# Attention with a routed expert layer: the rest of the routing ahead of the next expert's splits, two early transposes moved, and register loads placed elsewhere

## The chip, the core and the metric

The kernel runs on one core of one Trainium2 chip. A core has a matrix engine (TensorE, "PE" in the profile; its weight loads are "PEld"), VectorE ("DVE"), ScalarE ("ACT"), GpSimd ("POOL") and SyncE ("SP"), which here issues most transfers. Each engine runs its own queue in order and waits for the others by semaphores. The metric is the device time of one execution in microseconds (us); lower is better.

## What is computed

Block attention over 4 batches, 8 heads, 768 positions and 64 channels gives x of 3072 rows and 512 columns. Each row is then sent to one of 8 experts, a two-layer network with 1024 hidden columns. The cut reference of that second part:

```python
logits = x @ w_gate                       # 8 experts
local_gate = sigmoid(x @ w_local)
for b in range(B):
    prev_e = -1
    for s in range(S):
        fresh_e = argmax(logits[b, s])
        e = fresh_e if s == 0 or local_gate[b, s] < 0.5 else prev_e
        prev_e = e
        p = softmax(logits[b, s])
        h = maximum(x[b, s] @ w1[e], 0)
        out[b, s] = p[e] * (h @ w2[e])
```

The expert of a row is known only at run time, so the kernel sorts rows by expert while it runs.

## The kernel before

**Slots.** Rows are sorted into slots of 128 rows, all of one expert. Slots 0 to 5 (`EARLY` = 6) are filled from the first batch alone, with its commonest expert, so that their work can begin before the routing of the other batches is known. Up to 38 more follow, and two small slots of at most 32 rows (the "few" path) whose first and last matrices are loaded plain into the tile `raw`. A slot's rows are fetched by an indirect transfer that GpSimd issues (`gather`, L1030, tile `xg`), transposed by TensorE (L1041, in `tx`) and split by ScalarE and VectorE into a high and a low part (`split_ps`, L1034 and L1036, tile `xT`). Results are scaled by the gate value `psort` and scattered by GpSimd (L1083).

**Matmuls.** Every product is made of three: high by high, high by low, low by high. `pair` does two slots (first layer L1180 to L1182, 12 matmuls per 128 hidden columns), `quad` four (L1197 to L1199). The second layer, `second`, is a loop of blocks (slots) and 8 steps each; a step is three matmuls of 512 columns (L1059 to L1061). Steps are counted over all blocks: 0 to 15 in a pair, 0 to 31 in the quad. Behind a step the function may call `mids[step]`, and at steps given by `PW1` and `PW2` the functions that replace the weights by those of the next expert: ScalarE rounds (L1013, tile `h`), VectorE and GpSimd subtract (L1016 and L1021, tile `l`); when a matrix is through, SyncE reloads its staging tile `stg` (L1008). In the first pair `PM0` names the steps of the transposes of slots 2 to 5; in the quad `PM4` those of slots 6 to 9, counted from 18.

**Routing.** `route`, `finish` and `rows` are generators of small VectorE instructions. They end in `words`, a row of integers on one partition that say which slot begins a new expert, which expert it is, and how many slots there are. Last of all comes `bp` (L995): three products of the one-hot tile `eqp` with the three parts of the gate values, then 24 matmuls with `A` (L999) and a sum (L1002) that give `psort` for slots 6 onward. A sibling of the L999 matmuls, L908, gives the rows' addresses.

**What sets the order.** The program is written out in one order, which fixes each engine's own. While the first pair and the quad are written, `flow` is called behind each step: it keeps an estimate of TensorE's and VectorE's time and gives out a routing instruction when, by that estimate, it would not start too early. `small(n)` instead gives out VectorE instructions for a credit of n at once, stopping at one for TensorE unless told otherwise. Each weight split adds 1.4 us to VectorE's estimated time (`self.dve(1.4)` in `split`), so routing behind it is given out later.

**Reading words.** `reg` (L1324, through `values_load`) makes each named engine load one word into a register (TENSOR_LOAD in the trace); conditions are taken on it. The words on the two small slots are loaded by all engines behind the quad (`some`), and the number of slots (`nb`) before the last slots.

Of the kernel before, what the change touches and what calls it, by code (L numbers as in the profile page):

```python
# [32 lines left out]
KT, FT = DM // P, DF // P  # L33
# [8 lines left out]
SLOTS = 44  # L42
# [2 lines left out]
FEW = 32  # L45
FEWS = 2
COLS = SLOTS + FEWS
FEW_AT = ((1, 26, 29, 36, 40, 57), (37, 59, 62, 76, 80, 98))
OOB = 4096
WARM = 44  # L50
# [11 lines left out]

SPLIT_BY = ("VGVV", "VGVG")

PM, PM0, PM4 = (2, 5), (3, 6, 11, 14), (18, 21, 24, 27)
PW1, PW2 = (0, 2, 4, 6), (10, 12, 14, 15)

ON_PE = {"PE": 2, "PE late": 4, "ACT": 4}
# [9 lines left out]
class Kernel:  # L78
    def __init__(self, ctx, tc, qT, kT, vT, vW, maskc, identc, wgc, w1, w2, c32c, cb16c, out):
# [46 lines left out]
        self.zero = cst.tile([P, P], F32, name="zero")  # L126
        self.words = cst.tile([1, 2 * COLS + 1], I32, name="words")
        self.gidx = cst.tile([P, COLS], I32, name="gidx")
        self.sidx = cst.tile([P, COLS], I32, name="sidx")
        self.psort = cst.tile([P, COLS], F32, name="psort")  # L130
        self.wz = cst.tile([P, P], BF16, name="wz")
# [653 lines left out]
    def finish(self):  # L785
# [191 lines left out]
        for i in range(2):  # L977
            nc.tensor.matmul(out=m[0:1, COLS * i:COLS * i + COLS], lhsT=w2[:, i:i + 1], rhs=self.ident[:, 0:COLS],
                             start=True, stop=True)
        yield "DVE"  # L980
        v.tensor_copy(out=self.words[:, 2 * COLS:], in_=tot)
        yield "DVE"
# [259 lines left out]
    def run(self):  # L1242
# [45 lines left out]
        def freed():  # L1288
            st["free"] += 1
            ask_rows()  # L1290
# [6 lines left out]
        def block0():  # L1297
            self.mw2 = self.pool("m_wk2")
            self.w2c = ExitStack()
            self.w2b = self.w2c.enter_context(tc.tile_pool(name="w2b", bufs=1))  # L1300
            self.xT = self.mw2.tile([P, KT, 2, 4, P], F32R, name="xT")
            self.hT = [self.mw2.tile([P, FT, 2, 2 * P], F32R, name="hT0")]
            for i in range(2):
                while st["next"] <= i:
                    self.small(1, True)
                    ask_rows()
                self.tx(i, "s")
                freed()
                yield
# [13 lines left out]
        def reg(i, engines, hi):  # L1323
            return nc.values_load(self.words[0:1, i:i + 1], engines=engines, min_val=0, max_val=hi)  # L1324

        def refill(w, nxt):

            with tc.If(nxt > 0):
                e = nc.s_assert_within(nxt - 1, 0, E - 1, skip_runtime_bounds_check_because="the branch is taken for 1 to E alone")
                for h in range(2):  # L1330
                    self.fetch(st["stage"][w][:, 2048 * h:2048 * h + 2048], w, 2048 * h, 2048 * h + 2048, e)

        def split(w, chunks):
            for q in chunks:
                eng = nc.vector if SPLIT_BY[w][q] == "V" else nc.gpsimd
                self.split(w, q * CH, q * CH + CH, st["stage"][w][:, q * CH:q * CH + CH], eng)

        def calls(n, mids={}):

            r = {}  # L1340

            def start(s):
                while "words" not in st:
                    self.small(1, True)
                if s not in r:
                    r[s] = reg(s, (ENG.SP, ENG.Activation, ENG.DVE, ENG.Pool), 1), reg(COLS + s, (ENG.SP,), E)
                return r[s]

            def weights(w, s, chunks):
                if not EARLY <= s < SLOTS:  # L1350
                    return
                new, nxt = start(s)
                with tc.If(new > 0):  # L1353
                    split(w, chunks)
                    if chunks[-1] == NCH - 1:
                        refill(w, nxt)

            def turn(u):
                while st["next"] <= u:
                    self.small(1, True)  # L1360
                if u % 2 and u >= 2 * PAIRS:
                    with tc.If(reg(u, (ENG.PE, ENG.Activation, ENG.DVE), 1) > 0):
                        self.tx(u)
                else:
                    self.tx(u)
                freed()

            mids = {j: lambda u=u: turn(u) for j, u in mids.items() if u < SLOTS}
            return mids, lambda *chunks: weights(0, n, chunks), lambda *chunks: weights(1, n, chunks)
# [11 lines left out]
        first = chain(block0(), self.pair(0, *calls(2, dict(zip(PM0, range(2, 6))))))  # L1381
# [5 lines left out]
        with ExitStack() as ctx:  # L1387
# [31 lines left out]
                        p = slice(2048 * h, 2048 * h + 2048)  # L1419
                        self.fetch(self.raw[:, p], w, p.start, p.stop, e)  # L1420

            rest = chain(first, self.quad(2, *calls(6, dict(zip(PM4, range(6, 10))))))
            while self.steps:
                next(rest, None)
                self.flow(C_T)
# [5 lines left out]
            self.raw = lw.tile([P, KT * DF], F32, name="raw")  # L1431
            few_load(0, 0)
            nc.vector.tensor_copy(out=self.four.rearrange("p (q t) -> p q t", q=4), in_=self.ident[0:FEW, 0:FEW].unsqueeze(1).to_broadcast([FEW, 4, FEW]))
            some = [reg(SLOTS + j, mybir.ALL_ENGINES, 1) for j in range(FEWS)]

            def few(j, part):
                with tc.If(some[j] > 0):
                    part(j)
                    if part == self.few_1:
                        few_load(j, 1)  # L1440
                    elif part == self.few_3 and j + 1 < FEWS:
                        few_load(j + 1, 0)

            steps = {}
            for j in range(FEWS):
                for n, part in zip(FEW_AT[j], (self.few_rows, self.few_turn, self.few_index)):
                    steps[n] = lambda j=j, part=part: part(j)
                for n, part in zip(FEW_AT[j][3:], (self.few_1, self.few_2, self.few_3)):
                    steps[n] = lambda j=j, part=part: few(j, part)
# [7 lines left out]
            def slots(i0, i1, n=0):  # L1457
                for i in range(i0, i1, 2):
                    c = i, i + 2, dict(zip(PM, (i + 4, i + 5)))
                    if i < 2 * PAIRS:  # L1460
                        n = run(self.pair(i, *calls(*c[1:])), n)
                    else:
                        slot(*c)
# [9 lines left out]
                    self.single(i, *calls(*c))  # L1473

            slots(EARLY, LATE)
            nb = reg(2 * COLS, mybir.ALL_ENGINES, SLOTS)
            self.yl, self.il, self.pl = lw.tile([P, 512], F32, name="yl"), fw.tile([P, 1], I32, name="il"), fw.tile([P, 1], F32, name="pl")
            nc.vector.memset(self.il, OOB)
            nc.vector.memset(self.pl, 0.0)
# [110 lines left out]
```

## Time and profile before

| | us |
|---|---|
| median of 3 runs | 429.3 |
| lowest, highest | 428.98, 429.51 |
| the profiled execution | 430.12 |
| its span | 428.3 |
| TensorE busy in it | 408.3 (95%) |
| VectorE, GpSimd, ScalarE busy | 225.7, 193.6, 180.5 |
| granted TensorE clock, mean | 0.992 |

The profile shows one execution. Its parts: up to about 130 us the attention, then the first pair's second layer and the quad, from 198 us the slots sorted by expert, in pairs. A busy TensorE is not a TensorE at its peak; matmul ends are modelled, so distances are taken here from start to start. The granted clock is a share of full speed (2.4 GHz). "Idle before" is the time in which an engine stood before an instruction, and the name behind it says what ended it.

### The profile page before, as it was taken

To read this page: it belongs to the slowest core of one execution; us is meant where nothing else is said; L and a number is where in the kernel's file an instruction comes from. 1 tells how busy PE (TensorE), PEld (TensorE's weight loads), DVE (VectorE), ACT (ScalarE), POOL (GpSimd) and SP (SyncE) were. 2 spreads that over 40 slices of the span, in tenths; PEclk is the share of its full clock that TensorE was granted. 3 is DMA by queue.
4 is the path that set the end of the run, shared out by engine and by line. 5 is a ranking of instruction groups with operands and counts; after the bars stand their busy time and mean duration, and the time that the engine had idled before them with its cause. 6 is when DMAs were issued, how large, how long until landed. Compare 5 with 4: busy or idle time off the path is not lost. (4 is left out here: it accounts for less than half of the span.)

```text
span 428.3 us, 11331 instructions
## 1 busy us (share of the span) xinstructions
PE 408.3 (95%) x4120; PEld 348.2 (81%) x4120; DVE 225.7 (53%) x486; ACT 180.5 (42%) x429; POOL 193.6 (45%) x290
## 2 busy tenths in 40 slices
PE   7889999999999999998999999999999999999993
PEld 6668877778798787877989888798998898979882
DVE  5678978989696678683222222225421732212631
ACT  3978877778863222272201102115520831111540
POOL 4398867776588200457521210214652560000570
PEclk9999999999999999998999999999999999999998
DMA  8999999998671102938766254401752291000010
GB/s 303 417 407 408 408 401 414 401 413 343 198 282 41 66 1 62 412 108 307 253 252 229 57 222 145 160 27 29 301 199 84 83 363 57 28 28 27 2 54 31
DMA packets 21958, 85.89 MB, mean 201 GB/s; under 512 B 2639, under 2 KB 3153, under 8 KB 18801
## 3 DMA queue, kind: packets, MB, share of 16 engines
q1 hardware_dynamic: 17600, 70.46, 42.7%
q0 software_dynamic: 4128, 14.22, 9.6%
q8 instruction: 39, 0.64, 0.6%
q14 instruction: 47, 0.38, 0.3%
q10 hardware_dynamic: 144, 0.20, 0.2%
HBM read 71.40 MB, written 13.60 MB: 198 GB/s over the span
## 5 line engine op out<-in xcount | busy, mean ns | idle before, releaser
L1180 PE MATMUL bs<-xT,h 128*128 128x256 f32 x288 | 82.6, 287 | 0.0
L1165 ACT ACTIVATE hT<-bs 128x512 fp32r<-128x512 f32 (+1 forms) x52 | 27.7, 532 | 129.0 <-PE bs L1182 109.3
L1181 PE MATMUL bs<-xT,h 128*128 128x256 f32 x288 | 81.7, 284 | 0.0
L1182 PE MATMUL bs<-xT,l 128*128 128x256 f32 x288 | 81.6, 283 | 0.0
L1059 PE MATMUL ba<-h,hT 128*128 128x512 f32 x192 | 78.1, 407 | 0.3
L1061 PE MATMUL ba<-h,hT 128*128 128x512 f32 x192 | 75.2, 392 | 0.0
L1060 PE MATMUL ba<-l,hT 128*128 128x512 f32 x192 | 75.0, 391 | 0.0
L1167 DVE SCALAR_TENSOR_TENSOR hT<-bs,hT 128x512 fp32r<-128x512 f32 (+1 forms) x52 | 31.6, 608 | 77.3 <-ACT hT L1165 67.6
L1030 POOL DMA_INDIRECT xg<-x_dram,gidx x26 | 30.3, 1166 | 83.4 <-POOLq L1353 28.6
L1083 POOL DMA_INDIRECT out_dram<-yo,sidx x22 | 23.9, 1088 | 80.0 <-DVEq L1353 29.1
L1180 PEld LDWEIGHTS bs<-xT,h 128*128 128x128 f32 x288 | 55.5, 193 | 1.4 <-issue 1.0
L1181 PEld LDWEIGHTS bs<-xT,h 128*128 128x128 f32 x288 | 55.5, 193 | 0.5 <-issue 0.2
L1182 PEld LDWEIGHTS bs<-xT,l 128*128 128x128 f32 x288 | 55.3, 192 | 0.0
L346 ACT ACTIVATE pr<-bs,nm 128x120 f32<-128x120 f32 x192 | 52.2, 382 | 5.1 <-DVE nm L342 4.9
L1021 POOL TENSOR_TENSOR l<-stg,h 128x256 fp32r<-128x256 f32 x48 | 40.6, 880 | 19.8 <-ACT h L1013 13.0
L1061 PEld LDWEIGHTS ba<-h,hT 128*128 128x128 f32 x192 | 36.0, 188 | 8.2
L1059 PEld LDWEIGHTS ba<-h,hT 128*128 128x128 f32 x192 | 36.1, 188 | 7.6 <-issue 0.7
L1060 PEld LDWEIGHTS ba<-l,hT 128*128 128x128 f32 x192 | 36.2, 189 | 6.3
L280 POOL COPY vw<-gs 24x444 f32<-24x444 f32 (+1 forms) x56 | 29.4, 553 | 18.1 <-issue 12.8
L1013 ACT CAST h<-stg 128x1024 fp32r<-128x1024 f32 x32 | 32.4, 1050 | 6.3 <-PE ba L1061 2.9
L367 PE MATMUL ba<-vw,pt 121*64 121x74 f32 x768 | 32.1, 231 | 1.3 <-POOL vw L280 0.8
L367 PEld LDWEIGHTS ba<-vw,pt 121*64 121x64 f32 x768 | 27.2, 136 | 6.5 <-issue 3.8
(267 smaller groups left out, 657.2 us busy)
## 6 DMA issues: line engine op xcount, KB each, us to landing
stg<-in_w SPq DMA_DIRECT2D x16, 1024.0 KB, 6.3
vw<-in_vW SPq DMA_DIRECT2D x16, 888.0 KB, 10.5
raw<-in_w SPq DMA_DIRECT2D x8, 1024.0 KB, 5.9
x_dram<-xs SPq DMA_DIRECT2D x8, 876.0 KB, 7.1
kp<-in_kT SPq DMA_DIRECT2D x16, 384.0 KB, 11.2
q<-in_qT SPq DMA_DIRECT2D x16, 384.0 KB, 10.5
vt<-in_vT SPq DMA_DIRECT2D x16, 384.0 KB, 9.9
wst<-in_w SPq DMA_DIRECT2D x8, 512.0 KB, 10.8
```

What stands on the lines that cost most here:

```text
L346: nc.scalar.activation(out=pr[:, h, u, :], in_=sp[:, h, u, :], func=AF.Exp, bias=nm[:, h, u:u + 1], scale=1.0)
L367: nc.tensor.matmul(out=ap[64 * c:64 * c + 64, u, h, :], lhsT=pt[0:W + 1, h, u, 64 * c:64 * c + 64], rhs=vw[n % NVW][0:W + 1, 2 * (NG * g + ...
L1013: self.nc.scalar.copy(out=hi, in_=src)
L1021: eng.tensor_tensor(out=lo[:, p], in0=src[:, p], in1=hi[:, p].bitcast(F32), op=ALU.subtract)
L1030: self.nc.gpsimd.indirect_dma_start(out=t.rearrange("p a d -> p (a d)"), out_offset=None, in_=rows, in_offset=bass.IndirectOffsetOnAxis(ap ...
L1059: nc.tensor.matmul(out=ps, lhsT=ah, rhs=wh, start=first, stop=False)
L1060: nc.tensor.matmul(out=ps, lhsT=ah, rhs=wl, start=False, stop=False)
L1061: nc.tensor.matmul(out=ps, lhsT=al, rhs=wh, start=False, stop=last)
L1167: self.nc.vector.scalar_tensor_tensor(out=l, in0=ps, scalar=0.0, in1=h.bitcast(F32), op0=ALU.max, op1=ALU.subtract)
L1180: nc.tensor.matmul(out=ps[:, j], lhsT=wh, rhs=xh[k], start=(k == 0), stop=False)
L1181: nc.tensor.matmul(out=ps[:, j], lhsT=wh, rhs=xl[k], start=False, stop=False)
L1182: nc.tensor.matmul(out=ps[:, j], lhsT=wl, rhs=xh[k], start=False, stop=(k == KT - 1))
```

## The change

Three things are changed in the program's order; nothing is computed otherwise.

1. Behind step 15 of the quad's second layer (`2 * FT - 1`), one step ahead of the first weight split, `small(30)` gives out whatever VectorE instructions of the routing stand next, up to the next one for TensorE.
2. `PM0` becomes (3, 6, 9, 12): the transposes of slots 4 and 5 are written behind steps 9 and 12 of the first pair's second layer instead of 11 and 14.
3. The words for the two small slots are loaded by all engines behind step 20 of the quad and the number of slots behind step 23 (`ASK`); the later places use the registers.

```diff
+ASK = ((20, (SLOTS, SLOTS + 1)), (23, (2 * COLS,)))
...
-PM, PM0, PM4 = (2, 5), (3, 6, 11, 14), (18, 21, 24, 27)
+PM, PM0, PM4 = (2, 5), (3, 6, 9, 12), (18, 21, 24, 27)
...
-            rest = chain(first, self.quad(2, *calls(6, dict(zip(PM4, range(6, 10))))))
+            mids, *more = calls(6, dict(zip(PM4, range(6, 10))))
+            mids[2 * FT - 1] = lambda: self.small(30)
+            known = {}
+            for n, r in ASK:
+                mids[n] = lambda r=r: known.update({i: reg(i, mybir.ALL_ENGINES, SLOTS if i == 2 * COLS else 1) for i in r})
+            rest = chain(first, self.quad(2, mids, *more))
...
-            some = [reg(SLOTS + j, mybir.ALL_ENGINES, 1) for j in range(FEWS)]
+            some = [known[SLOTS + j] for j in range(FEWS)]
...
-            nb = reg(2 * COLS, mybir.ALL_ENGINES, SLOTS)
+            nb = known[2 * COLS]
```

Lines of the changed kernel stand one further down (L996 is L995), and six from L1427 on.

VectorE in the second half of the quad, before: a product `bp`, then a weight split `l` (of the tile `stg`), a row split `xT`, and the second `bp`.

```order
L990 TENSOR_TENSOR eqp<-c_82,blk 128x960
L995 TENSOR_TENSOR bp<-eqp,p_87 128x24x40
L1324 TENSOR_LOAD words
L1353 COMPARE_AND_BRANCH
L1016 TENSOR_TENSOR l_2481<-stg_2782,h_2479 128x1024
L1353 UNCONDITIONAL_BRANCH x2
L1036 TENSOR_TENSOR xT<-bt,xT 128x4x128
L1353 COMPARE_AND_BRANCH
L1353 UNCONDITIONAL_BRANCH x2
L995 TENSOR_TENSOR bp<-eqp,p_87 128x24x40
```

The second `bp` stands behind a weight split and a row split.

VectorE at the end of the quad, before: the last weight split, the third `bp`, the sum for `psort`.

```order
L1016 TENSOR_TENSOR l_2482<-stg_2783,h_2480 128x1024
L1353 UNCONDITIONAL_BRANCH x2
L1353 COMPARE_AND_BRANCH
L1328 UNCONDITIONAL_BRANCH
L1353 UNCONDITIONAL_BRANCH
L995 TENSOR_TENSOR bp<-eqp,p_87 128x24x40
L1417 UNCONDITIONAL_BRANCH
L1002 TENSOR_REDUCE psort<-bt 128x40
L1433 COPY four<-ident 32x128
```

The third stands behind the last weight split of the quad.

VectorE in the second half of the quad, now (the words are loaded into registers).

```order
L991 TENSOR_TENSOR eqp<-c_82,blk 128x960
L996 TENSOR_TENSOR bp<-eqp,p_87 128x24x40 x3
L1325 TENSOR_LOAD words
L1354 COMPARE_AND_BRANCH
L1017 TENSOR_TENSOR l_2481<-stg_2782,h_2479 128x1024
L1354 UNCONDITIONAL_BRANCH x2
L1037 TENSOR_TENSOR xT<-bt,xT 128x4x128
L1354 COMPARE_AND_BRANCH
L1354 UNCONDITIONAL_BRANCH x2
L1325 TENSOR_LOAD words x2
L1354 COMPARE_AND_BRANCH
L1017 TENSOR_TENSOR l_2481<-stg_2782,h_2479 128x1024
```

The three `bp` follow each other, and the first weight split comes behind them; the loads of the two words stand behind the first row split.

TensorE at the end of the quad, before: the last steps, then the first of the 24 matmuls on `bp` and `A`.

```order
L1060 MATMUL ba_3374<-l_2482,hT_2789 128x512
L1061 MATMUL ba_3374<-h_2480,hT_2789 128x512
L1059 MATMUL ba_3374<-h_2480,hT_2789 128x512
L1060 MATMUL ba_3374<-l_2482,hT_2789 128x512
L1061 MATMUL ba_3374<-h_2480,hT_2789 128x512
L1353 UNCONDITIONAL_BRANCH
L999 LDWEIGHTS A
L999 MATMUL bt<-bp,A 128x120
L999 LDWEIGHTS A
L999 MATMUL bt<-bp,A 128x120
```

Behind the last step comes the block of matmuls for `psort`, and behind that the next pair.

TensorE within the quad's third block, now, around step 20.

```order
L1060 MATMUL ba<-h_2480,hT_2789 128x512
L1354 UNCONDITIONAL_BRANCH
L1061 MATMUL ba<-l_2482,hT_2789 128x512
L1062 MATMUL ba<-h_2480,hT_2789 128x512
L1354 UNCONDITIONAL_BRANCH
L1325 TENSOR_LOAD words x2
L1060 MATMUL ba<-h_2480,hT_2789 128x512
L1061 MATMUL ba<-l_2482,hT_2789 128x512
L1062 MATMUL ba<-h_2480,hT_2789 128x512
L1042 MATMUL bt<-ident,xg_110 128x128 x4
```

The two loads stand ahead of step 21 and the transposes of slot 7 (`xg`). TensorE around step 23, now.

```order
L1060 MATMUL ba<-h_2480,hT_2789 128x512
L1061 MATMUL ba<-l_2482,hT_2789 128x512
L1062 MATMUL ba<-h_2480,hT_2789 128x512
L1060 MATMUL ba<-h_2480,hT_2789 128x512
L1354 UNCONDITIONAL_BRANCH
L1061 MATMUL ba<-l_2482,hT_2789 128x512
L1062 MATMUL ba<-h_2480,hT_2789 128x512
L1000 LDWEIGHTS A
L1000 MATMUL bt<-bp,A 128x120
L1000 LDWEIGHTS A
L1000 MATMUL bt<-bp,A 128x120
```

The matmuls on `bp` stand behind step 23, with eight steps of the quad behind them.

TensorE in the first pair's second layer, before, around the transposes of slot 4.

```order
L1060 MATMUL ba_2859<-l_2482,hT_2529 128x512
L1061 MATMUL ba_2859<-h_2480,hT_2529 128x512
L1059 MATMUL ba_2859<-h_2480,hT_2529 128x512
L1060 MATMUL ba_2859<-l_2482,hT_2529 128x512
L1061 MATMUL ba_2859<-h_2480,hT_2529 128x512
L1059 MATMUL ba_2859<-h_2480,hT_2529 128x512
L1060 MATMUL ba_2859<-l_2482,hT_2529 128x512
L1061 MATMUL ba_2859<-h_2480,hT_2529 128x512
L1041 MATMUL bt<-ident,xg_2787 128x128 x4
L1059 MATMUL ba_2859<-h_2480,hT_2529 128x512
```

They stand behind step 11. The same rows now.

```order
L1061 MATMUL ba_2859<-l_2482,hT_2529 128x512
L1062 MATMUL ba_2859<-h_2480,hT_2529 128x512
L1042 MATMUL bt<-ident,xg_2787 128x128 x4
L1060 MATMUL ba_2859<-h_2480,hT_2529 128x512
L1061 MATMUL ba_2859<-l_2482,hT_2529 128x512
L1062 MATMUL ba_2859<-h_2480,hT_2529 128x512
L1060 MATMUL ba_2859<-h_2480,hT_2529 128x512
L1061 MATMUL ba_2859<-l_2482,hT_2529 128x512
L1062 MATMUL ba_2859<-h_2480,hT_2529 128x512
L1060 MATMUL ba_2859<-h_2480,hT_2529 128x512
```

Six rows of matmuls (two steps) changed sides with the transposes of slot 4; those of slot 5 moved in the same way.

## Rows read from the trace of the kernel before

**Rows 1.** Waits of TensorE, whole span: who waited for whom, total us, times, longest.
```profile
PE bt L999 <- DVE bp L995: 2.1, 1, 2.1
...
PE bs L1198 <- DVE xT L1036: 0.2, 1, 0.2
```

**Rows 2.** The same view from 200 us to the end, all of it.
```profile
PE bs L1136 <- issue: 0.2, 1, 0.2
```

**Rows 3.** Timeline of TensorE: start, length, instruction, count, idle before and releaser.
```profile
193.35 0.40 PE L1061 MATMUL ba<-h,hT 128*128 128x512 f32 x1
195.85 2.58 PE L999 MATMUL bt<-bp,A 128*128 128x120 bf16 x24 [2.10 <-DVE bp L995]
198.19 0.56 PE L1180 MATMUL bs<-xT,h 128*128 128x256 f32 x1
...
199.32 0.28 PE L1182 MATMUL bs<-xT,l 128*128 128x256 f32 x1
199.43 0.28 PE L1180 MATMUL bs<-xT,h 128*128 128x256 f32 x1
```

**Rows 4.** Stretch: length, busy by engine, granted clock, DMA share, GB/s.
```profile
195.85:199.30 3.45, 3.45 (x29) 3.45 (x30) 0.40 (x2) 0.00 (x0) 2.81 (x3) 0.52 0.99 411
```

**Rows 5.** Timeline of VectorE in and behind the quad.
```profile
179.87 1.16 DVE L995 TENSOR_TENSOR bp<-eqp,p 128x960 bf16<-128x960 f32 x1
182.10 1.23 DVE L1016 TENSOR_TENSOR l<-stg,h 128x1024 fp32r<-128x1024 f32 x1 [1.08 <-ACT h L1013]
...
184.59 1.15 DVE L995 TENSOR_TENSOR bp<-eqp,p 128x960 bf16<-128x960 f32 x1
...
194.64 1.15 DVE L995 TENSOR_TENSOR bp<-eqp,p 128x960 bf16<-128x960 f32 x1
```

**Rows 6.** Timeline of TensorE: the sibling of the L999 matmuls, and the next matmul.
```profile
172.92 1.03 PE L908 MATMUL bt<-bt,A 128*128 128x80 bf16 x24
173.79 0.48 PE L1059 MATMUL ba<-h,hT 128*128 128x512 f32 x1
```

**Rows 7.** Timeline of TensorE: last matmul of the first pair, third of the quad.
```profile
144.88 0.40 PE L1061 MATMUL ba<-h,hT 128*128 128x512 f32 x1
...
146.31 0.39 PE L1199 MATMUL bs<-xT,l 128*128 128x512 f32 x1
```

**Rows 8.** Stretch behind the gathers of slots 4 and 5, columns as in rows 4.
```profile
140.00:140.40 0.40, 0.40 (x4) 0.31 (x3) 0.40 (x1) 0.00 (x0) 0.39 (x1) 1.00 0.00 0
```

**Rows 9.** Loads of words by TensorE's queue, 358 to 364: ns min/median/max, first and last start.
```profile
L1324 PEldq TENSOR_LOAD <-words x1: 301/301/301, 359.4 to 359.4; - x1
```

**Rows 10.** Timeline of TensorE around that load.
```profile
359.60 0.39 PE L1061 MATMUL ba<-h,hT 128*128 128x512 f32 x1
359.83 0.39 PE L1059 MATMUL ba<-h,hT 128*128 128x512 f32 x1
...
363.23 0.28 PE L1180 MATMUL bs<-xT,h 128*128 128x256 f32 x1
```

**Rows 11.** Timeline of GpSimd: its weight splits, and the gather for the few path.
```profile
189.71 3.86 POOL L1021 TENSOR_TENSOR l<-stg,h 128x256 fp32r<-128x256 f32 x4
...
206.23 2.85 POOL L1021 TENSOR_TENSOR l<-stg,h 128x256 fp32r<-128x256 f32 x4
209.23 0.88 POOL L1088 DMA_INDIRECT xm<-x_dram,gidx  x1 [0.16 <-issue]
```

**Rows 12.** Line L1008 on SyncE, 211 to 213 us: ns, starts; us from issue to landing.
```profile
L1008 SPq DMA_DIRECT2D raw<-in_w x2: 333/338/342, 211.3 to 211.9; - x2
...
DMA to landing us min/median/max: 9.8/9.8/9.8
```

**Rows 13.** Tile `xg`, 130 to 240 us: landing of its gathers.
```profile
DMA to landing us min/median/max: 4.0/5.3/6.5
```

**Rows 14.** Timeline of TensorE: the few path's transposes and its first matmuls on `raw`.
```profile
218.76 0.42 PE L1097 MATMUL bt<-ident,xm 32*128 32x32 f32 x4
...
226.15 1.93 PE L1117 MATMUL bs<-raw,xf 128*32 128x256 f32 x32
```

## The prediction

> **What bounds the kernel now.** I read first who TensorE waited for, over the whole span and then from 200 us on. After 200 us it waits 0.2 us in all [rows 2]: the experts' matmuls stand end to end for the last 220 us, so whatever is won or lost before 200 us reaches the end undiminished, unless a transfer that now lands in time becomes late. Over the whole span its longest single wait is the 2.1 us of the L999 matmuls (they sort the gate values by slot) for VectorE's product bp at L995; a smaller one, at L1198, is for the split of the last transposed early rows [rows 1].
>
> Next I looked at the instructions around the first wait. The last matmul of the four blocks (slots 2 to 5) starts at 193.35; matmuls of this kind follow each other every 0.23 us [rows 10], so TensorE is free at 193.58. L999 begins at 195.85, when the third bp ends: 194.64 + 1.15 [rows 3, 5]. So the hole is 195.85 - 193.58 = 2.27 us. Behind it the granted clock is 0.52 until 199.3 [rows 4], almost all of it the lower level, 1.2 GHz; it was idle before it fell. That is a second price of the same wait.
>
> On VectorE the three bp stand at 179.87, 184.59 and 194.64 [rows 5]: a split of the next expert's weights (L1016, 1.2 us) is ahead of the second, and four more splits and all four row splits are ahead of the third. None of these feeds bp; the order alone makes it late.
>
> **First edit: VectorE's rest of the routing ahead of the splits.** It adds no arithmetic. The three bp, back to back from the start of the first, now end about 179.87 + 3 x 1.16 = 183.3 [rows 5]. TensorE reaches the L999 matmuls behind step 23 of the second layer of the four blocks, whose steps are numbered 0 to 31. Eight steps of three matmuls, 8 x 0.7 = 5.6 us, and two transposes of 0.35 each (estimated as one and a half matmuls) lie between there and 193.58, so it is there at about 187.3: 4 us in hand.
>
> What it takes away:
> - the hole, 2.27 us;
> - L999 at the low clock: 198.19 - 195.85 = 2.34 us [rows 3]. At full clock half of that is 1.17; the other bound is the sibling at L908, 24 matmuls of 80 columns in 173.79 - 172.92 = 0.87 us [rows 6], which for 120 columns gives 1.30. I take 1.2, since half the measured time is the same instruction: 1.1 us gained;
> - the first five matmuls of the next pair, 199.32 - 198.19 = 1.13 us instead of 5 x 0.12 = 0.60 [rows 3]: 0.5 us gained.
>
> Together 3.9 us (3.8 to 3.95 by the two bounds).
>
> What it moves: the first split of the next expert starts when the bp end, 183.3 instead of 182.10, 1.2 us later. On VectorE this is given back, since the second bp (1.15 us) no longer stands at 184.59; by 186 the two orders are level. The new expert's weights are first read by the pair of slots 6 and 7, at about 194. The third bp leaves VectorE's tail, where only splits remain. What is late next? GpSimd ends its share of the first matrix at 193.57 (189.71 + 3.86) and of the second at 209.08 (206.23 + 2.85) [rows 11]. The pair needs the first after 24 of its matmuls, about 194 + 24 x 0.12 = 197, and the second only after 96 x 0.12 + 18 x 0.23 = 15.7 us, about 209.8, plus two transposes. Both are in time, the second by a microsecond or so.
>
> **Second edit: early rows transposed sooner.** The transposes of slots 4 and 5 go from steps 11 and 14 of the second layer of the first pair to steps 9 and 12, each two steps of three matmuls, 1.4 us, earlier. TensorE's work is the same. It now loses time at the start of the four blocks: the matmul at 144.88 should be followed by three at 0.23, the third at 145.58; it is at 146.31 [rows 7]. That is 0.73 us, put down to VectorE's split of slot 5 [rows 1]. With that split 1.4 us earlier the wait is gone. Its cover: the rows must have been gathered. The transposes would be at about 140.1 and 142.6 (from 145.11, the end of step 15, less two steps, less a transpose of 0.35, less 1.4; and three steps and a transpose before that), and the core's DMA engines move nothing more in the 0.4 us from 140.0 on [rows 8], so both gathers have arrived, the first with little room. On VectorE the row splits pass one more piece of a one-hot tile (L662), which TensorE first reads 27 us later, for the matmuls at 172.92 [rows 6]. Bounds 0 and 0.73; I take 0.73, as nothing else is late at 145.
>
> What comes behind follows: VectorE's routing runs between the results of the four blocks' first layer, and the weight loads and gathers hang on the routing, so they too come about 0.7 us sooner. A small wait that TensorE has for a gathered block further on stays as it is.
>
> **Third edit: deciding words read within the four blocks.** Three register loads per engine move, two from the head of the next pair and one from near the end, to steps 20 and 23. On TensorE's queue a load lasts 0.30 us [rows 9]. The one at 359.4 was executed while the matmul that stands behind it began at 363.23, with the matmuls under it at their usual 0.23 [rows 9, 10]: TensorE's queue runs 3.5 us or more ahead, so a load is hidden as long as no wait has emptied that lead. Bounds: 0, and 3 x 0.30 = 0.9 us with no lead. I take 0. Nothing is gained at the end either, because TensorE does not wait there [rows 2]. On SyncE the loads stand ahead of weight reloads that wait for GpSimd's splits anyway; on ScalarE and GpSimd they pass between casts, gathers and scatters, 0.6 us in one place, with rows due two steps later.
>
> The Trainium skill ("DMA: Bandwidth & Descriptors", section "Latency and other measured facts") puts a floor of about 600 ns under a tensor_load. The row here is half of that, so the measurement decides; by the page three unhidden loads would be 1.8 us instead of 0.9 us, and with the lead seen here still nothing.
>
> **The sum.** 3.9 + 0.7 + 0 = 4.6 us. The profiled execution took 430.12 us, 428.3 of span and 1.8 around it; less 4.6 is 425.5. It lies 0.8 above the median of the three runs, 429.3; against the median the sum gives **424.7 us**.
>
> **The rivals.**
> - *The feeds of the few-row path become the wait.* TensorE comes 4.6 us earlier, GpSimd and the DMA queues only 0.7. The transposes of these rows (218.76) move to 214.2 and the first matmuls on the plain weights (226.15) to 221.6 [rows 14]. The rows' gather is issued at 209.23 [rows 11]; gathers land 4.0 to 6.5 us after issue [rows 13], at 213.2 to 215.7. The second half of the weights is issued at 211.9 and lands 9.8 us later, at 221.7 [rows 12]. Less the 0.7, both are at the edge: a loss of 0 to 1.5 us. For it: both margins are under a microsecond, and the next rows' gathers now compete earlier. Against: those bytes are moved either way. I take 0.6: 425.3.
> - *The loads show.* If the wait for a gathered block, just ahead of step 20, empties TensorE's lead, 0.9 us: 425.6. Against: a matmul that waits in the queue lets the queue fill behind it.
> - *The second edit gives nothing* (the first gather late, or another wait under it): 425.4.
> - *The first edit doesn't do what it says.* If VectorE is not through with bp when L999 comes up, the wait only moves; with the second edit alone 428.6. Against: the 4 us in hand.
> - *Slower.* The plain weights' second half is held up by the rows' gathers. If it lands at 224.6 TensorE stands for 3.0 us, and with the low clock behind it (1.1 + 0.5, as at 195.85) the gain of 4.6 is spent; from 225.5, 3.8 us later than now, the kernel is slower by 3.9 + 1.6 - 4.6 = 0.9 us or more, 430.2. Against: the engines would have to lose a third of 10 us of transfer to 0.6 MB that they carry now too.
>
> **How the numbers follow.** Forecast 424.7 with chance 0.63; few-row feeds 425.3, 0.18; loads 425.6, 0.06; second edit void 425.4, 0.06; first void 428.6, 0.04; slower 430.2, 0.03. The measurement can tell about 0.2%, 0.9 us: below 428.4 is faster, which all but the last two are, 0.93; 428.6 counts as the same, 0.04; slower 0.03. The range: down from 424.7 by 0.3 for the spread of the runs (428.98 to 429.51) and 0.4 for small waits that I leave as they are, should they shrink too: 424.0. Up to the middle of the feeds' price and its own spread, 425.3 + 0.9 = 426.2. It leaves out some 0.1 to 0.15.
>
> **What would show it.** In the profile of the changed kernel: the three bp in a row before the first L1016 of the next expert; the psort matmuls in about 1.2 us amid the four blocks with no wait ahead; full granted clock from 130 us to the end of the matmuls; the pair of slots 6 and 7 starting near 194; no gap at the start of the four blocks; loads of words amid matmuls at an unbroken 0.23. I am wrong if TensorE's waits from 200 us on grow by over a microsecond, at L1097 or L1117 first, or if the clock falls again.

## The result, and the profile of the changed kernel

The changed kernel takes 424.02 us in the median of 4 runs (423.53 to 424.6), the kernel before 429.14 (427.14 to 429.51): 0.9891 of it, 95% interval 0.9857 to 0.9925. Predicted were 424.7 and a range of 424.0 to 426.2, so it lies at the lower edge of the range. The profiled execution took 423.69 us, with a span of 421.9 (before: 430.12 and 428.3). The same code was measured twice more beside the experiments, on two chips: 0.9924 (0.9908 to 0.994) and 0.9908 (0.9889 to 0.9927) of the kernel before.

TensorE's waits from 130 us to the end, all of them: the rows that answer to [rows 1] for the two waits that the prediction spoke of are gone, and from 200 us on, where [rows 2] had one, there is none.

```profile
engine line waited for: us in total, times, longest us
PE bt L1042 <- DMA xg<-x_dram,gidx: 0.2, 1, 0.2
```

VectorE in the quad, answering to [rows 5] (start, length, instruction, count): the three `bp` in a row, and the first weight split behind them.

```profile
177.97 3.34 DVE L996 TENSOR_TENSOR bp<-eqp,p 128x960 bf16<-128x960 f32 x3
181.24 1.21 DVE L1017 TENSOR_TENSOR l<-stg,h 128x1024 fp32r<-128x1024 f32 x1
```

TensorE's timeline at the sorting matmuls and at the start of the pair of slots 6 and 7, answering to [rows 3].

```profile
184.84 0.40 PE L1062 MATMUL ba<-h,hT 128*128 128x512 f32 x1
185.08 1.43 PE L1000 MATMUL bt<-bp,A 128*128 128x120 bf16 x24
186.33 0.48 PE L1060 MATMUL ba<-h,hT 128*128 128x512 f32 x1
...
192.66 0.40 PE L1062 MATMUL ba<-h,hT 128*128 128x512 f32 x1
192.89 0.28 PE L1181 MATMUL bs<-xT,h 128*128 128x256 f32 x1
193.01 0.27 PE L1182 MATMUL bs<-xT,h 128*128 128x256 f32 x1
...
193.47 0.28 PE L1183 MATMUL bs<-xT,l 128*128 128x256 f32 x1
```

The 24 matmuls start 0.24 us behind their forerunner, as any matmul there does, take 186.33 - 185.08 = 1.25 us, and the next pair begins 0.23 us behind the quad's last step, 0.12 us from matmul to matmul. The stretches (length, busy by engine, granted clock, DMA share, GB/s), answering to [rows 4], show full clock in each:

```profile
180.00:186.00 6.00, 5.76 (x43) 4.45 (x42) 5.16 (x7) 4.82 (x7) 1.82 (x2) 1.00 0.34 109
186.00:192.80 6.80, 6.80 (x42) 5.66 (x40) 3.61 (x4) 4.13 (x6) 6.22 (x6) 1.00 0.31 95
192.80:200.00 7.20, 7.20 (x62) 7.15 (x61) 2.77 (x5) 2.82 (x4) 6.37 (x7) 1.00 0.97 368
200.00:417.00 217.00, 214.21 (x1470) 188.35 (x1469) 69.50 (x103) 55.16 (x78) 70.94 (x76) 1.00 0.37 131
```

The start of the quad, answering to [rows 7]: last matmul of the pair, then the quad's first three, 0.23 us apart.

```profile
143.76 0.39 PE L1062 MATMUL ba<-h,hT 128*128 128x512 f32 x1
143.98 0.39 PE L1198 MATMUL bs<-xT,h 128*128 128x512 f32 x1
144.21 0.39 PE L1199 MATMUL bs<-xT,h 128*128 128x512 f32 x1
144.44 0.39 PE L1200 MATMUL bs<-xT,l 128*128 128x512 f32 x1
```

**Where the 6.4 us between the two profiles went.** I laid the traces side by side, matmul by matmul. From the last matmul of the pair to the third of the quad it is 144.44 - 143.76 = 0.68 us, where it was 146.31 - 144.88 = 1.43: 0.75 less. From there to the next pair it is 192.89 - 144.44 = 48.45 us, where it was 198.19 - 146.31 = 51.88: 3.43 less; and the next pair's first five matmuls take 193.47 - 192.89 = 0.58 instead of 199.32 - 198.19 = 1.13: 0.55 less. That is 4.7. Some 1.1 us were gained by 111 us, in attention code that is the same in both, and 0.6 around the few path's L1136. The traces of the experiments, with whatever edits, are 0.1 to 1.1 us earlier than the profiled execution of before at 111 us, and all of them are 0.57 us shorter at L1136 (2.21 us from the matmul ahead of it to the one behind it, instead of 2.78). So what is gained at L1136 belongs to the one execution of before, and the 1.1 us at 111 us lie within what executions of the same code differ by.

### The profile page after: what moved, and what is told of

Read it like the earlier page. It is cut to its first block, busy times and chain, and to the rows that moved or that the text cites. A ratio compares the mean times of both kernels' runs of the same rounds, so it can differ in the third digit from the quotient of the medians.

```text
span 421.9 us, 11332 instructions
## 1 busy us (share of the span) xinstructions
PE 404.2 (96%) x4120; PEld 346.1 (82%) x4120; DVE 224.8 (53%) x486; ACT 180.0 (43%) x429; POOL 193.1 (46%) x290
## 5 line engine op out<-in xcount | busy, mean ns | idle before, releaser
L1031 POOL DMA_INDIRECT xg<-x_dram,gidx x26 | 29.4, 1131 | 78.3 <-PE ba L1062 27.5
L1084 POOL DMA_INDIRECT out_dram<-yo,sidx x22 | 24.8, 1128 | 77.6 <-DVEq L1354 29.2
```

Of the source, the lines that this page charges most:

```text
L1031: self.nc.gpsimd.indirect_dma_start(out=t.rearrange("p a d -> p (a d)"), out_offset=None, in_=rows, in_offset=bass.IndirectOffsetOnAxis(ap ...
```

## The experiments

Ratios are to the kernel before on the same chip, with 95% intervals. Its own times differ from chip to chip (medians 428.59, 427.73 and 428.26 us in the three sets below), for a reason that the experiments show.

### Each edit by itself

The first edit alone:

```diff
+            mids, *more = calls(6, dict(zip(PM4, range(6, 10))))
+            mids[2 * FT - 1] = lambda: self.small(30)
-            rest = chain(first, self.quad(2, *calls(6, dict(zip(PM4, range(6, 10))))))
+            rest = chain(first, self.quad(2, mids, *more))
```

> The kernel before with the first edit alone (VectorE's rest of the routing ahead of the weight splits). My theory: the hole of 2.27 us ahead of L999 goes, and with it 1.1 us of L999 and 0.5 us of the next matmuls at the low clock: 3.9 us off 429.1, 425.2 (ratio 0.991); the granted clock stays at 1.00 from 185 to 200 us and no wait is left at the sorting matmuls. If the first edit were void the time would be 429.1. If the feeds of the few-row path become the wait, TensorE waits 0.5 to 1.5 us between 212 and 224 us, 425.8 to 426.7.

Measured: 425.08 us (424.65 to 425.88), 0.9922 (0.99 to 0.9944), 3.5 us off. No wait for `bp` and no wait at the few path is in the trace; the clock is 1.00 from 186 us on.

The second alone:

```diff
-PM, PM0, PM4 = (2, 5), (3, 6, 11, 14), (18, 21, 24, 27)
+PM, PM0, PM4 = (2, 5), (3, 6, 9, 12), (18, 21, 24, 27)
```

> The kernel before with the second edit alone (slots 4 and 5 transposed behind steps 9 and 12). My theory: the 0.73 us at the start of the four blocks go and all behind moves up by as much, the wait at L999 keeping its 2.1 us: 428.4 (ratio 0.9983). If another wait stands under it (the gathered rows late, or VectorE's routing no earlier than before, so that the wait at L999 grows to 2.8 us): 429.1.

Measured: 428.25 us (426.26 to 429.09), 0.9987 (0.9967 to 1.0006). The times alone can't tell 0.73 from nothing, and beside the first edit they show nothing of it (below: 425.10 with both, 425.08 with the first alone). In the trace the quad's third matmul comes 0.7 us earlier against its forerunners, and the wait at L999 stays 2.10 us: the mechanism is there at its predicted size, and what it is worth at the end is not shown by the times.

The third alone (`ASK` and `known` of the change, with the old `PM0` and without `small(30)`):

> The kernel before with the third edit alone (the words read behind steps 20 and 23 of the four blocks). My theory: nothing, 429.1 within 0.3 us, because TensorE's queue runs ahead and hides its loads, and VectorE, GpSimd and SyncE have room. If the loads show, 0.3 to 0.9 us more, 429.4 to 430.0, with a matmul distance over 0.5 us near 182 to 188 us. If the reading at its old place cost something, the pair behind the four blocks starts sooner behind L999: 0.3 to 0.6 us less.

Measured: 428.82 us (427.43 to 429.91), 1.0007 (0.9991 to 1.0024): no gain, and no loss that can be told. Its profiled execution, 427.68, held a surprise. The same wait stands before the sorting matmuls in this trace, in that of the second edit alone and in that of before, and behind it there are three different things. Timeline of TensorE in the kernel with the third edit alone:

```profile
195.59 1.43 PE L1000 MATMUL bt<-bp,A 128*128 128x120 bf16 x24 [2.09 <-DVE bp L996]
196.84 0.36 PE L1181 MATMUL bs<-xT,h 128*128 128x256 f32 x1
197.04 0.28 PE L1182 MATMUL bs<-xT,h 128*128 128x256 f32 x1
```

and in the kernel with the second alone, with the stretch behind it:

```profile
194.96 1.44 PE L999 MATMUL bt<-bp,A 128*128 128x120 bf16 x24 [2.10 <-DVE bp L995]
196.27 0.48 PE L1180 MATMUL bs<-xT,h 128*128 128x256 f32 x1
196.55 0.41 PE L1181 MATMUL bs<-xT,h 128*128 128x256 f32 x1
```
```profile
194.90:196.20 1.30, 1.24 (x24) 1.24 (x24) 0.00 (x1) 0.00 (x0) 1.02 (x1) 1.00 1.02 422
196.20:200.50 4.30, 4.30 (x27) 4.29 (x25) 0.40 (x2) 0.00 (x0) 3.85 (x5) 0.60 1.00 400
```

In before the sorting matmuls themselves run at the lower level [rows 3, 4]. With the second edit alone they run at full speed (1.31 us) and the matmuls behind them at 1.2 GHz (0.21 us apart instead of 0.12), some 1.5 us lost in all: the first 16 take 3.48 us (196.27 to 199.75), with the third alone 1.99 (196.84 to 198.83). With the third alone the clock does not fall at all behind the wait. The wait is 2.1 us in all three.

So the low clock behind the wait is no fixed price. For each execution its mean granted clock is known, and the times of kernels with the wait go with it. A stretch such as the 3.45 us at 0.52 in [rows 4] takes 0.004 off the mean of 428 us. The mean also counts the end of the program, where the clock falls too (0.94 from 400 us on in the profiled execution of before, 0.86 in that of the filled wait below), so 0.993 parts the executions only roughly:

| kernel | executions | clock 0.993 or less: how many, median us | above: how many, median us |
|---|---|---|---|
| before, first set | 23 | 16, 428.83 | 7, 427.45 |
| before, second set | 17 | 4, 428.47 | 13, 427.64 |
| before, third set | 11 | 6, 428.62 | 5, 428.06 |
| second edit alone | 12 | 8, 428.43 | 4, 426.59 |
| third edit alone | 12 | 8, 429.23 | 4, 427.94 |
| eight runs of kernels with the first edit and no other long wait | 46 | 1, 424.20 | 45, 423.3 to 426.2 |

Against the executions of before with the low clock the first edit alone gains 428.83 - 425.08 = 3.75 us, against the others 427.45 - 425.08 = 2.4 us. The prediction's 3.9 was the sum of a hole of 2.27 and a clock term of 1.6: the hole is found at its size, the clock term at 1.4 between the two groups here and 1.5 in the trace of the second edit alone, and it is paid in some executions only. Within the groups the second edit alone is 0.4 and 0.9 us faster than before and the third alone 0.4 and 0.5 slower: medians of few executions, which settle neither.

### The clock term by itself

The kernel before, with nine matmuls that need nothing from VectorE ahead of L999:

```diff
         m = self.bank("t")
+        for _ in range(9):
+            nc.tensor.matmul(out=m, lhsT=self.A[:, 0, :], rhs=self.A[:, 0:4, :].rearrange("p t s -> p (t s)"), start=True, stop=True)
```

> The kernel before with nine matmuls of 512 columns on static data (the tile A) put ahead of the L999 matmuls, so that TensorE works while it waits for bp; they write a bank that L999 then overwrites, and nothing of the output changes. My theory: the low clock behind the wait comes of the idle time, and the 2.27 us of the wait stay: in runs where before has the low clock (granted clock about 0.992 over the run) 1.6 us less, 427.0, in every run; its runs no longer fall into two groups, and L999 to the next pair take 1.25 us instead of 2.34. If L999 is slow for a reason of its own (its new weights for every matmul): 428.6 as before, two groups as before.

Measured: 427.23 us (426.74 to 427.86, 11 runs), 0.9989 (0.9977 to 1.0). Timeline of TensorE, the nine and the 24 (here at L1001), and the stretch from there on:

```profile
192.84 2.12 PE L999 MATMUL bt<-A 128*128 128x512 bf16 x9
195.09 1.42 PE L1001 MATMUL bt<-bp,A 128*128 128x120 bf16 x24
196.39 0.36 PE L1182 MATMUL bs<-xT,h 128*128 128x256 f32 x1
```
```profile
195.10:200.00 4.90, 4.90 (x54) 4.89 (x54) 0.40 (x2) 0.47 (x1) 4.24 (x5) 1.00 1.01 412
```

TensorE gets to its sorting matmuls no sooner, since `bp` is as late as before, but it isn't idle meanwhile, and the clock behind it is 1.00; 10 of the 11 executions are above 0.993, the eleventh is the profiled one, whose clock is 1.00 up to 400 us, and the slowest is 0.6 us faster than the median of before with the low clock on this chip (428.47). The sorting matmuls take 1.30 us here, and in two traces above 1.25 and 1.31 behind an idle wait: they are not slow by themselves. That the idle time brought the clock down, where it came down, is what all the counts point to: a mean of 0.993 or less in 42 of the 75 executions that stood idle ahead of L999, in 1 of the 46 without that wait. This experiment by itself is thin evidence, since on its chip only 4 of 17 executions of before had the low clock, and none of 11 could be chance. For the same reason the gain over before is only 0.5 us, not the 1.6 that was expected against the low clock.

### The first two edits, and all three

The change without its third edit:

```diff
+PM, PM0, PM4 = (2, 5), (3, 6, 9, 12), (18, 21, 24, 27)
+            mids[2 * FT - 1] = lambda: self.small(30)
```

> The changed kernel without its third edit. My theory: the same as the changed kernel, 424.0 (0.988 of before), since the third edit is worth nothing. If the reading in the four blocks takes something off the start of the next pair, this one is 0.3 to 0.9 us slower than the changed kernel; if its loads show on TensorE, as much faster.

Measured: 425.1 us (424.57 to 425.39), 0.9915 (0.9894 to 0.9936), no better than the first edit alone on the same chip. Its trace has a wait that neither before nor the changed kernel has. Waits of TensorE from 200 us on, and the timeline at the few path:

```profile
PE bs L1117 <- DMA raw<-in_w: 0.4, 1, 0.4
```
```profile
220.96 0.63 PE L1117 MATMUL bs<-raw,xf 128*32 128x256 f32 x4
222.01 1.92 PE L1117 MATMUL bs<-raw,xf 128*32 128x256 f32 x28 [0.43 <-DMA raw<-in_w]
```

The 32 matmuls take 223.86 - 220.96 = 2.9 us to the next matmul, instead of 1.9 in the changed kernel: the second edit's gain is lost here. That is the prediction's first rival, the feeds of the few path, in an actual execution. How GpSimd came to be late is seen in its timeline, this kernel first and the changed kernel second (idle before and its releaser in brackets):

```profile
198.09 2.83 POOL L1021 TENSOR_TENSOR l<-stg,h 128x256 fp32r<-128x256 f32 x4
204.00 1.02 POOL L1083 DMA_INDIRECT out_dram<-yo,sidx  x1 [3.09 <-DMA out_dram<-yo,sidx]
205.04 2.82 POOL L1021 TENSOR_TENSOR l<-stg,h 128x256 fp32r<-128x256 f32 x4
208.02 0.88 POOL L1088 DMA_INDIRECT xm<-x_dram,gidx  x1 [0.16 <-POOLq L1353]
```
```profile
197.47 2.83 POOL L1022 TENSOR_TENSOR l<-stg,h 128x256 fp32r<-128x256 f32 x4
201.59 1.01 POOL L1084 DMA_INDIRECT out_dram<-yo,sidx  x1 [1.29 <-DMA out_dram<-yo,sidx]
202.63 2.83 POOL L1022 TENSOR_TENSOR l<-stg,h 128x256 fp32r<-128x256 f32 x4
205.62 0.88 POOL L1089 DMA_INDIRECT xm<-x_dram,gidx  x1 [0.16 <-issue]
```

A scatter waits, on a semaphore of the program, for the landing of the scatter before it: in all thirteen traces without the eight loads it starts 0.8 us behind that landing, also where the profile names something else. Behind it on GpSimd's queue stand the last split of the second matrix and the gather `xm`; SyncE's loads of `raw` stand behind a reload of the tile that the split reads. So the whole feed of the few path hangs on when one scatter lands beside a reload of 2 MB. GpSimd waited 3.1 us for it here, 1.3 us there.

The changed kernel on another chip, beside the two edits with the few path's work four steps later, and all three edits with the same delay:

```diff
-FEW_AT = ((1, 26, 29, 36, 40, 57), (37, 59, 62, 76, 80, 98))
+FEW_AT = ((1, 26, 29, 40, 44, 57), (37, 59, 62, 76, 80, 98))
```

> The changed kernel once more, on the chip of the next three. The first two edits without the third came to 425.1 there where before came to 428.6 (0.9915), the changed kernel to 0.9891 of before elsewhere. If the third edit is worth something beside the other two: 423.9 (0.989 of before). If the difference lay in the chip or the runs: 425.0 (0.9915).

> The first two edits, and TensorE's work on the first few rows (L1117, and L1125 behind it) four steps, about 2.8 us, later. In the trace of the two edits alone TensorE lost 0.8 us at L1117, where the plain weights landed at 221.97, too late by that much. If that wait is what hides the second edit, and what sets these two edits apart from all three: 424.3 (0.990 of before), with no wait for raw. If it is not in most runs, or the difference has another cause: 425.1, no change.

> The changed kernel with the work on the first few rows four steps later. Its own trace shows no wait for raw (1.4 us of margin), so by my theory nothing: the time of the changed kernel on this chip within 0.3 us, and the runs at most closer together. If the weights come late in part of its runs too, 0.3 to 0.8 us less.

Measured: 424.48 us (0.9924, 0.9908 to 0.994), 424.58 (0.9925, 0.9908 to 0.9942) and 424.27 (0.9919, 0.9903 to 0.9936). The three are the same. With the first rows' work four steps later the wait for `raw` is gone in the traces of both, and two edits are as good as three; for all three edits the delay brings nothing, as expected. In the last trace another feed was late instead, for a reason of its own: the gather went out at 206.15 us, no later than in most other traces, and took 7.6 us to land, where it took 5.3 in the changed kernel.

```profile
PE bt L1098 <- DMA xm<-x_dram,gidx: 0.6, 1, 0.6
```

Then both once more, on one chip:

> The changed kernel, beside the two edits alone on one chip. If the third edit is worth nothing: the two within 0.3 us of each other, both about 424.5. If it is worth the 1 us by which the two edits alone lagged on another chip: this one 1 us ahead.

> The first two edits without the third, again. If the third edit is worth nothing: 424.5 as its neighbour with all three, and a wait for raw at L1117 in some executions at most. If reading the words early is worth something: 425.5, with the wait for raw of 0.4 us or more in the trace again.

Measured: 424.28 us (423.26 to 425.06), 0.9908 (0.9889 to 0.9927), and 424.83 (424.1 to 425.88), 0.9918 (0.9901 to 0.9935). The medians lie 0.55 us apart in favour of all three, and the intervals overlap. The trace of the two edits alone has a wait at the few path again, this time for the gathered rows, and not that of all three:

```profile
PE bt L1097 <- DMA xm<-x_dram,gidx: 0.5, 1, 0.5
```

So the third edit is worth between nothing and some 0.5 us beside the first two by the medians, and the runs don't settle whether it is worth anything.

### Room left in the second and the third edit

The transposes of slots 4 and 5 still earlier:

```diff
-PM, PM0, PM4 = (2, 5), (3, 6, 9, 12), (18, 21, 24, 27)
+PM, PM0, PM4 = (2, 5), (3, 6, 7, 8), (18, 21, 24, 27)
```

> The changed kernel with the rows of slots 4 and 5 transposed behind steps 7 and 8 instead of 9 and 12. The rows landed at 137.75 and 139.35 us in the changed kernel, and TensorE would be at these transposes at 137.55 and 138.6. My theory: there is no room left for moving them further; TensorE waits 0.2 and 0.7 us for them, 0.8 to 1.0 us slower than the changed kernel, 425.4. If the rows were there well before the trace's landing: no difference, 424.5.

Measured: 425.16 us (424.59 to 426.17), 0.9932 (0.9914 to 0.995), 0.9 us more than all three edits on the same chip. Waits of TensorE from 130 us on:

```profile
PE bt L1042 <- DMA xg<-x_dram,gidx: 0.9, 2, 0.7
```

The sum and the longer of the two waits are as worked out from the landings, so those are when the rows are really there. Steps 9 and 12 stand behind that with little to spare: in the changed kernel the rows land at 137.75 and 139.35, and it transposes them at 138.96 and 141.48.

More loads on TensorE's queue:

```diff
+            ask = mids[20]
+            def more_loads():
+                ask()
+                for _ in range(8):
+                    nc.values_load(self.words[0:1, SLOTS:SLOTS + 1], engines=(ENG.PE,), min_val=0, max_val=1)
+            mids[20] = more_loads
```

> The changed kernel with eight more loads of a word on TensorE alone, behind step 20 of the four blocks. In the changed kernel the two loads there stand on TensorE's queue from 180.69 to 182.07 (0.64 us of it a wait for VectorE's third bp, then 0.42 us from load to load), and the matmul behind them starts at 182.54: only 0.4 us of cover are left. Eight more take 8 x 0.42 = 3.4 us: by this reading 3.0 us slower than the changed kernel, 427.5, more if the granted clock falls behind the gap. If the queue runs 3.5 us ahead here as it did at 359 us in the trace of before: 3.4 + 1.4 - 3.5 = 1.3 us slower, 425.8. If a load is hidden whatever its number: 424.5.

Measured: 431.53 us (430.53 to 432.62), 1.008 (1.0054 to 1.0106), 7.25 us more than all three edits on this chip: more than any of the theories gave. The loads on TensorE's queue (ns min/median/max, first and last start), its waits, and the stretches:

```profile
L1432 PEldq TENSOR_LOAD <-words x8: 299/302/572, 182.7 to 187.6; - x8
L1432 PEldq FUSED_REGOPS  x8: 146/146/167, 183.1 to 188.2; - x8
```
```profile
PE ba L1060 <- issue: 5.0, 1, 5.0
```
```profile
183.38:188.50 5.12, 0.16 (x1) 0.00 (x0) 1.58 (x2) 1.33 (x2) 3.09 (x3) 1.00 0.14 54
188.50:192.30 3.80, 3.79 (x12) 3.06 (x13) 0.69 (x1) 1.52 (x2) 3.42 (x5) 0.55 0.48 109
```

Two things were mis-sized. A load was taken at 0.42 us from one to the next; with the register operation and what else belongs to each it is (187.6 - 182.7) / 7 = 0.70, so eight take 5.6. And the hole of 5.0 us brought the clock down: 0.55 for the next 3.8 us, 1.7 us lost; all four executions have a mean clock of 0.990 or less. Some 0.5 of the 7.25 us stays unaccounted for. Of the theories the one with little cover is right: nearly all of the 5.6 us is seen.

Why the cover is little there shows in the changed kernel: its loads, and TensorE's matmuls around them.

```profile
L1325 PEldq TENSOR_LOAD <-words x3: 312/312/960, 180.7 to 185.4; - x3
```
```profile
180.65 0.66 PE L1042 MATMUL bt<-ident,xg 128*128 128x128 f32 x4 [0.24 <-DMA xg<-x_dram,gidx]
181.06 0.48 PE L1060 MATMUL ba<-h,hT 128*128 128x512 f32 x1
...
182.54 0.40 PE L1060 MATMUL ba<-h,hT 128*128 128x512 f32 x1
```

The first load stands behind step 20, two steps behind transposes that wait for gathered rows. It starts at 180.7, when they start, not earlier; the matmul behind it in the program starts at 182.54. In the kernel with the third edit alone it is the same, transposes at 182.42 and first load at 182.5:

```profile
182.42 0.66 PE L1042 MATMUL bt<-ident,xg 128*128 128x128 f32 x4 [0.29 <-DMA xg<-x_dram,gidx]
```
```profile
L1325 PEldq TENSOR_LOAD <-words x3: 304/310/657, 182.5 to 183.8; - x3
```

So the wait did use up the lead, as the second rival had it, down to 182.54 - 180.7 = 1.85 us; two loads, the first of 0.96 us with some wait for `bp` in it (0.66 in the kernel with the third edit alone, where VectorE's last `bp` ahead of it had ended at 180.86), were through at 182.07. They were hidden by less than 0.5 us, not by 2.

## Why the prediction came out right, point by point

**The first edit's hole: right.** 2.27 us predicted; against executions of before that kept their clock, 2.4 measured (medians of 6 and 7 executions). The three `bp` end at 181.31, the sorting matmuls start at 185.08 with 3.8 us in hand (4 predicted), the pair of slots 6 and 7 starts at 192.89 (194 predicted, less the 1.1 us that this execution was early).

**Its clock term: right in size, wrong in kind.** 1.1 + 0.5 us were read from one execution and taken for every one. Between the two groups of the table lie 0.6 to 1.8 us, and half of before's 51 executions there didn't pay it. The runs shown ahead of the prediction (428.98 to 429.51) are where the low-clock group lies (their own clocks are not on record), so the median that the sum was made against most likely carried the term, and 424.7 came out near. That is luck as far as this term goes. In the second and third set the same change gains 4.0 and 4.3 us against the executions of before with the low clock and 3.2 and 3.8 against the others, where the sum has 4.6 and, without the clock term, 3.0; against all of them it gains 3.25 and 4.0.

**The second edit: right at the place where it acts.** 0.73 predicted, 0.7 seen in the traces at the start of the quad; where a feed of the few path was late it was lost again 75 us on, and no time of a run shows it clear of the noise.

**The third edit: right as to nothing lost, for a thinner reason than given.** The lead of 3.5 us was read at a place with no wait before it [rows 9, 10]. Here it was 1.85 us, and two loads took 1.38 (180.69 to 182.07), so that the upper bound of 0.9 us for three was too low. The prediction's "a matmul that waits in the queue lets the queue fill behind it" doesn't hold for a load that stands behind it: the load doesn't run ahead of the wait. The Trainium skill ("Perfetto Trace Analysis", section "Sequencer Loop") has engine instructions pushed into a queue, where they wait for their semaphores, and control instructions started in microcode. If a load counts as a control instruction, it could by that have run while the transposes waited. The rows differ, and the measurement decides.

**The few path's feeds: the step that was mis-sized.** "TensorE comes 4.6 us earlier, GpSimd and the DMA queues only 0.7" does not hold for the changed kernel: there the gather `xm` goes out at 205.62 instead of 209.23 [rows 11], 3.6 us earlier, and the loads of `raw` at 207.7 and 208.3 instead of 211.3 and 211.9 [rows 12]. Some 1.1 us of it is that this execution was early as a whole (at 111 us); 2.5 are left. I had looked at GpSimd's splits and overlooked the scatter between them, which waits for the landing of the scatter before it: in the traces that landing is at 204.38 before and at 200.77 after. The 0.7 is near where that landing is late: reckoned in the same way, `xm` goes out 0.3 to 0.8 us earlier than before in three of the nine traces with the first edit (none of them has the third), and 1.3 to 2.7 in the other six. With the earlier landing the margins are 2.0 us at the transposes (212.96, rows landed at 210.92) and about 1.4 at the plain weights (220.35, landed at 218.98, of which the second half is read later still). The rival was none the less real: of the nine traces with the first edit (the one with eight more loads left aside), three show waits of 0.4 to 0.6 us there, two of them with the late landing. Its weight, 0.18, and its price, 0.6, were fair; its reason held in those two.

**The other rivals.** The first edit void, the second void and slower than before by a late `raw` were not seen in any trace.

**What the profile alone would have misled to.** The two profiles differ by 6.4 us; 1.7 of it lies in code and moments that the change doesn't touch.

## What to carry to other kernels

A wait of TensorE costs its length in every execution and a slower clock in some; before adding the second to a sum, look at the granted clock of several executions, not at the profiled one alone. Give out an engine's work in the order in which others wait for it: most of the gain came from instructions that needed nothing new and stood behind work that nobody was waiting for yet. And when a bottleneck moves forward by 4 us, follow each feed's queue back to what it waits for, scatters included, before saying that the feed stays where it was.

## What the runs showed of the hardware that was not expected

- One and the same idle time of 2.1 us on TensorE was followed by a low clock at once, after 1.3 us of work, or not at all, in three executions; 26 of 51 executions of one kernel had a mean granted clock of 0.993 or less. What decides it stays open.
- A load of a word on TensorE's queue doesn't run ahead of a matmul before it that waits; in all seven traces with loads behind step 20 it starts within 0.1 us of that matmul, and its cover is the work between the two.
- A transfer that shares the DMA engines with a large reload can have its last part land 1.6 to 1.7 us behind the rest, or not. In the first two edits alone 15 of the 16 completions of the scatter that GpSimd waits for came by 201.48, the last at 203.19; in the changed kernel all 16 came by 200.77. The traces hold one packet of 16 KB on the instruction queue near the start of that reload: in the five kernels with the first and the third edit (without the one with more loads) it starts 0.1 to 0.3 us before the reload is issued, and the scatter goes out 9.6 to 10.3 us behind the issue; in the four with the first edit and without the third it starts 0.1 to 0.6 us behind it, and the scatter goes out 10.4 to 11.9 us behind. That is a coincidence in nine traces, not a cause shown; it wasn't tried to move the packet by itself. It would explain why the third edit seemed to help.
